# Moving sums, plain products and the second sequence's differences in a fused Fourier mixing and squared-ReLU kernel

## The chip, the cores and the metric

The kernel runs on one core of a Trainium2 chip. The metric is the device time of one execution in microseconds (us); less is better. The engines are called as in the profile: PE (TensorE), PEld (its weight loads), DVE (VectorE), ACT (ScalarE), POOL (GpSimd) and SP, whose queue issues most DMAs.

## The reference

```python
# x: (8, 3008, 256) float32; w_in: (256, 2048); w_out: (2048, 256)
X = np.fft.fft(np.fft.fft(x, axis=1), axis=2).real
t = X.reshape(8 * 3008, 256)
h = t @ w_in
out = np.square(np.maximum(h, 0.0)) @ w_out
```

Eight sequences of 3008 rows are Fourier transformed along rows and columns, the real part goes through a layer of 2048 features with a squared ReLU, and back to 256 columns.

## The kernel before

**Fourier part.** A sequence is folded on its symmetries before TensorE transforms it: sums and differences of rows (`rows_of`: sums `fs`, differences `fd`), then of columns (`columns_of`: tile `sc`, its first half from `fs`, its second from `fd`), then the split by parity (`parities_of`, which reads both halves of `sc` with a copy on ACT and writes `w`), and further halvings (`even`, `odd`, `twice_*`, `order`). The transform (`dft_ops`) gives two tables `Pt` and `Qt` for the sequence. One column of all seven later sequences is folded and transformed by itself (`fold_columns`, whose data come by small DMAs into `xe`, and `dft_ops(None)`). For the folds ACT first copies one operand into a bank of PSUM (`spare`, pool `psh`, tag h), so DVE reads one operand there.

**Layer part.** The transform along the columns is folded into w_in (`G1`, `G2`, and `gE` for the odd column). A *step* is one sequence, one block of 252 frequencies and one pair j of feature chunks; there are 6 blocks of 8 steps a sequence, 48 steps a sequence, 384 in all, numbered from 0. A step's `front` makes hP and hQ on TensorE (L984), `he` and the two halves of `g` on DVE (L988, L990, L991), ReLU and square on ACT (L995, L998). Tiles hP, hQ, the folds' banks and the transforms' banks all take turns in the two banks of `psh`: each new one waits for the reader of the one before the last.

**Products with w_out.** Two steps make a pair. POOL forms sums of their `g` (`sums_even` in even steps, L1010 to L1012; `sums_odd` in odd ones, L1020 to L1027) in tile `s`, and 20 products of a third of a step's width do the work of the 8 full ones (24 thirds) of two plain steps: 12 in `first_half` (banks F0 to F2, run three steps after the pair's even step, so in odd steps), 8 in `second_half` (banks S0 to S2, one step later). They need sums of w_out's parts (`wsum`, and some parts of `wout` replaced in place), made by `sum_wout`: a copy on ACT (L381) and three to six additions on DVE (L384), for the four groups of `SUMS`, and for pairs 0 and 1 (`slice(0, 2)`) and 2 and 3 (`slice(2, 4)`) apart. The first block (steps 0 to 7) uses w_out itself (`plain`, banks mA and mB, L1074; copied out by `gather_plain`, L1084). Every eighth step `gather` (early, upper, lower, joins) combines the banks on DVE (L1103 to L1133), and `store` transposes on DVE and writes out.

**Order of the work.** Engines run their instructions in the order in which the program issues them. The start is written out by hand in `ORDER`: TS, PW, H, PR are the four stages that round a part of w_in or w_out (`w` in front of the number: DVE, ACT, DVE, POOL); `f8b` is the TensorE half of step 8's second half, `d8b` its split on DVE (L970 to L973), `rl` and `sq` ReLU and square, `bk` the plain products of a step, `cm` POOL's sums, `sum8` and `sum9` the first sums of w_out, `hi` joins of the first sequence's transform. From step `PLAIN` = 10 on a loop issues, for each step: front, sums of w_out (up to step 14), due parts of a gather, pieces of the next sequence's folds, stores, products, ReLU, square, POOL's sums. The next sequence's pieces come from `ahead` as a list of (cost, function); `share`, `pace` and `spent` say how many of them a step may take (`FIRST` in the first sequence, `SHARE` later; `ROOM` limits a step), and pieces of no cost are issued at the end of a step (`free_pieces`). The transforms' pieces are issued between a step's products.

The list for the second sequence (sequence 1) is, before: the turning factors, 12 folds, the folds of the odd columns, their transform, 19 folds, the transforms.

Of the kernel before, what the change touches and what calls it, by code (L numbers as in the profile page):

```python
# [15 lines left out]
P = 128  # L16
# [68 lines left out]
def kernel(  # L85
# [288 lines left out]
    def sum_wout(qs, shared):  # L374
# [3 lines left out]
        ps, held = spare(slice(0, P)), {}  # L378
# [75 lines left out]
    def fold_columns():  # L454
# [12 lines left out]
        def begin():  # L467
            s = hp.tile([P, 2, NL, NE], F32, name="es", tag="es", bufs=1)
            tt(out=s, in0=xe[:, 0::2], in1=xe[:, 1::2], op=ALU.add)
            for kp in range(2):  # L470
                tt(out=we[:, :, kp], in0=s[:, 0], in1=s[:, 1], op=ALU.subtract if kp else ALU.add)
# [17 lines left out]

        def copy_pairs():  # L490
# [3 lines left out]
            nc.scalar.copy(pair, we[r, v, 1])  # L494

        def twice_even():
            butterfly(we[r, 2:3, 0], we[r, 4:5, 0], one)
            for i, u in enumerate((5, 7)):
                mix(out=we[r, u, 0], in0=we[r, u, 0], scalar=by(BY_AB, COS), in1=f[:, i], op0=ALU.mult, op1=ALU.add)

        def twice_odd():
            butterfly(we[r, v, 1], we[r, w, 1], pair)
# [68 lines left out]
    def fold_later(b):  # L571
# [5 lines left out]
        def rows_of(t):  # L577
            r = rows(t)

            def f():  # L580
# [4 lines left out]
                tt(out=fd[t][r], in0=v[r, 0::3], in1=p, op=SUB)  # L585
                load_later(LATER.index((b, t)) + NX)

            return 1.3, f

        def columns_of(t):  # L590
            r = rows(t)

            def f():
# [6 lines left out]
                tt(out=sc[t][r, :, H + 1:D], in0=q, in1=fd[t][r, :, D - 1:H:-1], op=SUB)  # L600

            return 0.8, f
# [706 lines left out]
    FIRST = (1.6, 2.6, 0.2, 0.2, 0.9, 1.9, 1.6, 1.9)  # L1309
# [10 lines left out]
    def pieces():  # L1320
# [3 lines left out]
        room, count = ROOM[i % NJ] if i >= per else 2.8, 2  # L1324
# [8 lines left out]
    def piece_beside():  # L1333
# [35 lines left out]
    def sums_at(i):  # L1369
        j, shared = i - NJ, list(SUMS)  # L1370
        if j < 3:
            for k in ((0,), (1,), (2, 3))[j]:
                sum_wout(slice(0, 2), shared[k])
        else:
            sum_wout(slice(2, 4), shared[j - 3])
# [24 lines left out]
    def step(token):  # L1400
# [45 lines left out]
        elif what == "sum":  # L1446
            sums_at(int(nm))
# [12 lines left out]
    for i in range(PLAIN, len(steps) + 7):  # L1460
        if i < len(steps):
# [10 lines left out]
            if i < NJ + 7:  # L1472
# [104 lines left out]
```

## Time and profile before

| | |
|---|---|
| three runs | 1901.33, 1901.73, 1903.04 us; median 1901.73 |
| the profiled execution | 1901.05 us, span 1899.3 us, granted clock 0.997 |
| busy, share of the span | PE 98%, PEld 92%, DVE 78%, ACT 57%, POOL 76% |
| step 10 begins at | 100.12 us of the span |
| the first sequence's last step (47) begins at | 297.54 us |
| HBM | 41.54 MB read, 24.69 MB written |

A line of the timeline holds the start, the duration, the engine, the line of the code, the operation, what it writes and reads, how many instructions are merged, and in brackets the idle time ahead of it with what ended it. A line of the waits holds who waited for whom, the total in us, how many times, and the longest. In a group of instructions the busy time and the mean duration of one (ns) stand behind the bar. In the table by stretches each engine's busy time is followed by its instructions, and the last three columns are the granted TensorE clock, the DMA share and GB/s.

### The profile page before, as it was taken

What the parts mean: (1) busy time and instruction counts of PE and PEld (TensorE: products, weight loads), DVE (VectorE), ACT (ScalarE), POOL (GpSimd) and SP (SyncE); (2) the same over time, 40 slices, a digit from 0 to 9 for tenths busy, and PEclk for the clock granted to TensorE, in tenths of its full rate; (3) what the DMA queues carried; (4) which work ended last, traced back from release to release, by engine and by line L of the source; (5) the groups of instructions that cost most, each with busy time, mean ns of one, the idle gap of its engine ahead of it and who ended that gap; (6) DMA issues with size and microseconds to landing.
All of it is one profiled execution on the core that took longest, in us unless ns stands there. A gap on an engine that the chain in (4) does not pass through costs nothing.

```text
span 1899.3 us, 34013 instructions
## 1 busy us (share of the span) xinstructions
PE 1868.8 (98%) x11408; PEld 1755.3 (92%) x11408; DVE 1478.6 (78%) x3507; ACT 1083.0 (57%) x1612; POOL 1450.8 (76%) x2115
## 2 busy tenths in 40 slices
PE   9999999999999999999999999999999999999998
PEld 7678889999999999999999999999999999999997
DVE  8688877888778877888778887788877888766665
ACT  5865655666456654656555574566645656445453
POOL 4367667887788887878778887788778878787886
PEclk9999999999999999999999999999999999999999
DMA  6431101110011000111011110111001100000000
GB/s 196 116 43 32 40 14 42 48 34 15 20 45 51 23 20 20 51 40 29 23 32 31 45 31 15 32 45 48 15 15 45 39 14 19 16 22 15 20 20 23
DMA packets 151310, 68.46 MB, mean 36 GB/s; under 512 B 131143, under 2 KB 142881, under 8 KB 151136
## 3 DMA queue, kind: packets, MB, share of 16 engines
q1 hardware_dynamic: 150590, 65.74, 13.8%
q8 instruction: 91, 1.49, 0.3%
q14 instruction: 83, 0.68, 0.1%
q0 software_dynamic: 416, 0.43, 0.1%
q10 hardware_dynamic: 130, 0.12, 0.0%
HBM read 41.54 MB, written 24.69 MB: 35 GB/s over the span
## 4 chain that ended last, share of the span: by engine, by line
PE 86%; DVE 10%; ACT 2%; issue 1%; POOL 0%; DMA 0%; SPq 0%; DVEq 0%; ACTq 0%; POOLq 0%
PE F L1045 31%; PE S L1045 19%; PE hP L984 15%; PE hQ L984 15%; DVE he L988 2%; PE pd L837 1%; PE pd L714 1%; DVE g L990 1%; DVE g L991 1%; PE mA L1074 1%; PE mB L1074 1%; PE pd L811 1%; PE pg L344 1%; ACT sp L644 1%; PE ph L955 0%
## 5 line engine op out<-in xcount | busy, mean ns | idle before, releaser
L995 ACT ACTIVATE g<-g 128x1008 f32<-128x1008 f32 (+1 forms) x384 | 399.4, 1040 | 313.7 <-DVE g L991 306.0
L988 DVE SCALAR_TENSOR_TENSOR he<-ew,gE,hP 128x252 f32<-128x252 f32 (+1 forms) x748 | 321.2, 470 | 295.9 <-PE hP L984 295.7
L998 ACT ACTIVATE g<-g 128x1008 f32<-128x1008 f32 (+1 forms) x384 | 399.3, 1040 | 12.0
L984 PE MATMUL hP<-Pt,G 128*128 128x252 f32 (+1 forms) x1496 | 380.1, 377 | 8.0 <-DVE w L646 2.9
L984 PE MATMUL hQ<-Qt,G 128*128 128x252 f32 (+3 forms) x1496 | 380.3, 377 | 5.0 <-DVE Pt L749 1.0
L1045 PE MATMUL F<-s,wsum 128*128 128x168 f32 (+1 forms) x1504 | 337.5, 306 | 0.0
L1020 POOL TENSOR_TENSOR s<-g 128x168 f32<-128x168 f32 (+1 forms) x188 | 101.8, 542 | 299.0 <-ACT g L998 294.6
L984 PEld LDWEIGHTS hQ<-Qt,G 128*128 128x128 f32 (+1 forms) x1496 | 280.2, 190 | 48.1 <-ACT g L995 4.2
L1045 PE MATMUL S<-s,wsum 128*128 128x168 f32 (+1 forms) x1504 | 305.7, 305 | 0.0
L1045 PE MATMUL F<-g,wout 128*128 128x168 f32 (+1 forms) x1504 | 305.7, 305 | 0.0
L984 PEld LDWEIGHTS hP<-Pt,G 128*128 128x128 f32 x1496 | 265.2, 190 | 29.7 <-ACT sp L631 4.3
L990 DVE TENSOR_TENSOR g<-he,hQ 128x504 f32<-128x504 f32 (+1 forms) x374 | 253.2, 677 | 49.8 <-PE hQ L984 6.2
L1045 PE MATMUL S<-s,wout 128*128 128x168 f32 (+1 forms) x1504 | 281.2, 306 | 0.1
L1045 PE MATMUL F<-g,wsum 128*128 128x168 f32 (+1 forms) x1504 | 275.0, 305 | 0.0
L1045 PEld LDWEIGHTS S<-s,wsum 128*128 128x128 f32 x1504 | 249.5, 190 | 8.2
L991 DVE TENSOR_TENSOR g<-he,hQ 128x504 f32<-128x504 f32 (+1 forms) x374 | 250.5, 670 | 0.0
L1045 PEld LDWEIGHTS F<-s,wsum 128*128 128x128 f32 x1504 | 248.8, 190 | 0.3 <-issue 0.2
L1045 PEld LDWEIGHTS F<-g,wsum 128*128 128x128 f32 x1504 | 240.6, 190 | 8.1
L1045 PEld LDWEIGHTS F<-g,wout 128*128 128x128 f32 x1504 | 240.6, 190 | 0.0
L1045 PEld LDWEIGHTS S<-s,wout 128*128 128x128 f32 x1504 | 232.1, 190 | 0.7 <-POOL s L1027 0.3
L1026 POOL TENSOR_TENSOR s<-s 128x336 f32<-128x336 f32 (+1 forms) x188 | 168.6, 897 | 14.7
L1023 POOL TENSOR_TENSOR s<-s 128x336 f32<-128x336 f32 (+1 forms) x188 | 168.5, 896 | 14.7
(227 smaller groups left out, 2498.5 us busy)
## 6 DMA issues: line engine op xcount, KB each, us to landing
out_dram<-os SPq DMA_DIRECT2D x376, 56.0 KB
xt<-in_x_dram SPq DMA_DIRECT2D x39, 384.0 KB
xt<-in_x_dram SPq DMA_DIRECT2D x63, 128.0 KB
ew<-e_dram SPq DMA_DIRECT2D x39, 126.0 KB
out_dram<-os SPq DMA_DIRECT2D x288, 7.0 KB
raw<-in_moe_w_in_dram SPq DMA_DIRECT2D x16, 256.0 KB
raw<-in_moe_w_out_dram SPq DMA_DIRECT2D x16, 256.0 KB
xt<-in_x_dram SPq DMA_DIRECT2D x2, 512.0 KB
```

The source lines that it names most:

```text
L344: nc.tensor.matmul(pg, tab[:, i], win[j][:, i], start=i == 0, stop=i == 1)
L984: nc.tensor.matmul(to[:, h, 0:n], w[:, fs], v[:, ks], start=h == 0, stop=True, skip_group_check=True)
L988: nc.vector.scalar_tensor_tensor(out=t[:, h, 0:n], in0=window[b, k0][:, 0:n], scalar=gE[:, fc:fc + 1], in1=hP[:, h, 0:n], op0=ALU.mult, op ...
L990: tt(out=g[:, :, 0:n], in0=t[:, :, 0:n], in1=hQ[:, :, 0:n], op=ALU.add)
L991: tt(out=g[:, :, n:2 * n][:, :, ::-1], in0=t[:, :, 0:n], in1=hQ[:, :, 0:n], op=ALU.subtract)
L995: act(g[:, :, 0:2 * n], g[:, :, 0:2 * n], AF.Relu)
L998: act(g[:, :, 0:2 * n], g[:, :, 0:2 * n], AF.Square)
L1020: gt(out=s[:, 11], in0=b2[:, 0], in1=b1[:, 0], op=SUB)
L1023: gt(out=s[:, 4:6], in0=s[:, 4:6], in1=s[:, 10:11].to_broadcast([P, 2, tb]), op=SUB)
L1026: gt(out=s[:, 6:9:2], in0=s[:, 2:4], in1=s[:, 6:8], op=ADD)
L1045: nc.tensor.matmul(acc[nm][:, slot, 0:tb], w, v, start=q == 0 and nm not in begun, stop=q == NJ // 2 - 1, skip_group_check=True)
L1074: nc.tensor.matmul(acc[nm][:, 0:2 * n], wout[:, j, h, c], g[:, c, 0:2 * n], start=j == c == 0, stop=j == NJ - 1 and c == 1)
```

## The change

- In `ORDER`, the plain products of steps 6 and 7 move: `bk6` to right behind `f8a`, `bk7` (before issued in the loop at step 10) to behind `rl9`.
- The sums of w_out move. Those for pairs 0 and 1 are issued one group at a time from `d6a` on (`su0a`, `su1a`, `su2a`, `su3a`) instead of at steps 8 to 10; those for pairs 2 and 3 at `su1b`, at step 10 (groups 2 and 0) and at step 11 (group 3) instead of at steps 11 to 14. Their PSUM tile comes from pool `psd` (tag d, the banks of `ends_of` and later of S1 and S2) instead of `psh`.
- `fold_columns` runs on GpSimd, but for one shuffle on DVE and the copies and multiplications on ACT.
- For the second sequence alone, `fd` and the second half of `sc` are computed on GpSimd, both operands from SBUF; ACT's copy for the latter goes.
- The second sequence's list of pieces is woven anew, with lower costs for the changed ones, and `FIRST` and the limits on a step's pieces in the first sequence differ.
- In `second_half` the third product of bank S1 comes ahead of the two of S2.

```diff
 def sum_wout(qs, shared):
-        ps, held = spare(slice(0, P)), {}
+        ps, held = psd.tile([P, 2 * D], F32, name="sw", tag="d"), {}
...
 def fold_columns():
         def begin():
             s = hp.tile([P, 2, NL, NE], F32, name="es", tag="es", bufs=1)
-            tt(out=s, in0=xe[:, 0::2], in1=xe[:, 1::2], op=ALU.add)
+            gt(out=s, in0=xe[:, 0::2], in1=xe[:, 1::2], op=ADD)
             for kp in range(2):
-                tt(out=we[:, :, kp], in0=s[:, 0], in1=s[:, 1], op=ALU.subtract if kp else ALU.add)
+                gt(out=we[:, :, kp], in0=s[:, 0], in1=s[:, 1], op=SUB if kp else ADD)
...
+        def pair_up(v, w, a):
+            gt(out=v, in0=a, in1=w, op=ADD)
+            gt(out=w, in0=a, in1=w, op=SUB)
+        def even():
             nc.scalar.copy(a, we[r, first, 0])
-        def even():
-            butterfly(we[r, first, 0], we[r, other, 0], a)
+            pair_up(we[r, first, 0], we[r, other, 0], a)
...
+        def twice_even():
             nc.scalar.copy(one, we[r, 2:3, 0])
             for i, (u, k) in enumerate(((7, SIN), (5, LESS))):
                 nc.scalar.mul(f[:, i], we[r, u, 0], by(BY_AB, k))
+            for u in (5, 7):
+                nc.scalar.mul(we[r, u, 0], we[r, u, 0], by(BY_AB, COS))
+            pair_up(we[r, 2:3, 0], we[r, 4:5, 0], one)
+            gt(out=we[r, 5:8:2, 0], in0=we[r, 5:8:2, 0], in1=f, op=ADD)
...
-        return [(0.8, begin), (0.3, order), (0.0, copy_even), (1.0, odd), (0.5, even), (0.0, copy_pairs),
-                (0.9, twice_even), (0.5, twice_odd)]
+        return [(0.1, begin), (0.3, order), (0.1, odd), (0.1, even), (0.1, odd_sums), (0.1, twice_even), (0.1, twice_odd)]
...
 def rows_of(t):
                 tt(out=fs[t][r, :, 0:D], in0=v[r, 0::3], in1=p, op=ADD)
-                tt(out=fd[t][r], in0=v[r, 0::3], in1=p, op=SUB)
+                if b == 1:
+                    gt(out=fd[t][r], in0=v[r, 0::3], in1=v[r, 1:3], op=SUB)
+                else:
+                    tt(out=fd[t][r], in0=v[r, 0::3], in1=p, op=SUB)
                 load_later(LATER.index((b, t)) + NX)
-            return 1.3, f
+            return 0.7 if b == 1 else 1.3, f
...
 def columns_of(t):
                 nc.scalar.copy(p, fs[t][r, :, 0:H + 1])
-                nc.scalar.copy(q, fd[t][r, :, 1:H])
+                if b > 1:
+                    nc.scalar.copy(q, fd[t][r, :, 1:H])
                 sc[t] = next_halves()
                 tt(out=sc[t][r, :, 0:H + 1], in0=p, in1=fs[t][r, :, D:H - 1:-1], op=ADD)
-                tt(out=sc[t][r, :, H + 1:D], in0=q, in1=fd[t][r, :, D - 1:H:-1], op=SUB)
-            return 0.8, f
+                (tt if b > 1 else gt)(out=sc[t][r, :, H + 1:D], in0=q if b > 1 else fd[t][r, :, 1:H],
+                                      in1=fd[t][r, :, D - 1:H:-1], op=SUB)
+            return 0.8 if b > 1 else 0.45, f
...
 def second_half(...):
         run((("S0", 0, 8, s[:, 2]), ("S0", 1, (0, 1), s[:, 4]), ("S0", 2, (0, 2), s[:, 8]), ("S1", 0, (1, 0), s[:, 6]),
-             ("S1", 1, 11, s[:, 10]), ("S2", 0, 7, s[:, 7]), ("S2", 1, (1, 3), s[:, 5]), ("S1", 2, 10, s[:, 3])),
+             ("S1", 1, 11, s[:, 10]), ("S1", 2, 10, s[:, 3]), ("S2", 0, 7, s[:, 7]), ("S2", 1, (1, 3), s[:, 5])),
...
 def ahead(b):
-        if b == 1:
-            early = [(0.0, start), (0.0, take_turn), (0.5, make_turn)]
-            middle = [(0.0, scale_columns)] + fold_columns() + tables + dft_ops(None)
...
-        return early + one + middle + two + groups
+        head = [(0.0, start), (0.0, take_turn), (0.5, make_turn)] + one[:9]
+        return (head + woven(one[9:] + two[:5], [(0.0, scale_columns)] + fold_columns(), 1) + tables
+                + woven(two[5:], dft_ops(None), 2) + groups)
+    def woven(ops, others, each):
+        out, others = [], list(others)
+        for k in range(0, len(ops), each):
+            out += ops[k:k + each] + others[:1]
+            del others[:1]
+        return out + others
...
-    FIRST = (1.6, 2.6, 0.2, 0.2, 0.9, 1.9, 1.6, 1.9)
+    FIRST = (1.6, 2.8, 0.0, 0.0, 0.9, 1.9, 1.6, 1.9)
...
-        room, count = ROOM[i % NJ] if i >= per else 2.8, 2
+        room, count = ROOM[i % NJ] * (1.0 if i >= per else 1.3), 2 if i >= per else 3
...
 ORDER
-        'gE6 PRw4 d6b sq5 fe7 pgC7 gE7 TSw5 bk4 TSw6 PWw5 restQ GC7 d6a spl PWw6 Hw5 f7b PRw5 f7a TSw7 bk5 Hw6 '
-        'PWw7 d7b PRw6 rl6 d7a sq6 f8b Hw7 f8a rl7 d8a sq7 PRw7 d8b sum8 rl8 f9a sq8 hi8 f9b d9a cm8 bk6 '
-        'd9b rl9 sum9 sq9 hi9 cm9 '
+        'gE6 PRw4 d6b sq5 fe7 pgC7 gE7 TSw5 bk4 TSw6 PWw5 restQ GC7 d6a su0a spl PWw6 Hw5 f7b PRw5 f7a su1a TSw7 bk5 '
+        'Hw6 PWw7 d7b PRw6 rl6 su2a d7a sq6 f8b Hw7 f8a bk6 rl7 d8b su3a PRw7 sq7 d8a rl8 f9a sq8 hi8 f9b d9a cm8 '
+        'd9b rl9 bk7 sq9 su1b hi9 cm9 '
...
 the loop
-            if i < NJ + 7:
-                sums_at(i)
+            for k in {PLAIN: (2, 0), PLAIN + 1: (3,)}.get(i, ()):
+                sums_of_wout(k, 1)
...
-        if i == PLAIN:
-            back_at(NJ - 1)
-        elif at >= NJ and at < len(steps):
+        if at >= NJ and at < len(steps):
```

More of the change, by code (lines that the diff above doesn't have):

```diff
@@ L475, in order, with odd_sums @@
             nc.vector.stream_shuffle(v, v, REVERSE)
-        def copy_even():
+        def pair_up(v, w, a):
+            gt(out=v, in0=a, in1=w, op=ADD)
+            gt(out=w, in0=a, in1=w, op=SUB)
+        def even():
             nc.scalar.copy(a, we[r, first, 0])
-        def even():
-            butterfly(we[r, first, 0], we[r, other, 0], a)
+            pair_up(we[r, first, 0], we[r, other, 0], a)
         def odd():
             for i, u in enumerate((other, first)):
-                tt(out=m[:, 3 * i:3 * i + 3], in0=we[r, u, 1], in1=turned(SIN + i, u), op=ALU.mult)
+                gt(out=m[:, 3 * i:3 * i + 3], in0=we[r, u, 1], in1=turned(SIN + i, u), op=ALU.mult)
             for u in (first, other):
-                tt(out=we[r, u, 1], in0=we[r, u, 1], in1=turned(COS, u), op=ALU.mult)
-            tt(out=we[r, both, 1], in0=we[r, both, 1], in1=m, op=ALU.add)
-        def copy_pairs():
+                gt(out=we[r, u, 1], in0=we[r, u, 1], in1=turned(COS, u), op=ALU.mult)
+        def odd_sums():
+            gt(out=we[r, both, 1], in0=we[r, both, 1], in1=m, op=ADD)
+        def twice_even():
             nc.scalar.copy(one, we[r, 2:3, 0])
@@ L493, in copy_pairs, with twice_odd @@
                 nc.scalar.mul(f[:, i], we[r, u, 0], by(BY_AB, k))
-            nc.scalar.copy(pair, we[r, v, 1])
[L496 to L502, printed above, removed]
-        return [(0.8, begin), (0.3, order), (0.0, copy_even), (1.0, odd), (0.5, even), (0.0, copy_pairs),
-                (0.9, twice_even), (0.5, twice_odd)]
+            for u in (5, 7):
+                nc.scalar.mul(we[r, u, 0], we[r, u, 0], by(BY_AB, COS))
+            pair_up(we[r, 2:3, 0], we[r, 4:5, 0], one)
+            gt(out=we[r, 5:8:2, 0], in0=we[r, 5:8:2, 0], in1=f, op=ADD)
+        def twice_odd():
+            nc.scalar.copy(pair, we[r, v, 1])
+            pair_up(we[r, v, 1], we[r, w, 1], pair)
+        return [(0.1, begin), (0.3, order), (0.1, odd), (0.1, even), (0.1, odd_sums), (0.1, twice_even), (0.1, twice_odd)]
     folds = turns = 0
@@ L1180, in ahead @@
         tables = [(0.0, lambda tab=tab, t=t: part_table(tab, t)) for t in (TWO, ODD0) for tab in (cosT, sinT)]
-        if b == 1:
-            early = [(0.0, start), (0.0, take_turn), (0.5, make_turn)]
-            middle = [(0.0, scale_columns)] + fold_columns() + tables + dft_ops(None)
-        else:
-            early, middle = [], []
-            groups = [(0.0, start)] + groups
-        one, two = fold_later(b)
-        return early + one + middle + two + groups
+        one, two = fold_later(b)
+        if b > 1:
+            return one + two + [(0.0, start)] + groups
+        head = [(0.0, start), (0.0, take_turn), (0.5, make_turn)] + one[:9]
[7 more added lines that the diff above has]
+        return out + others
     pieces = [fold(t) for t in range(NT)]
@@ L1367, in front_at, with sums_of_wout @@
         return b, k0, n, j, made["g", i]
[L1369 to L1375, printed above, removed]
+    def sums_of_wout(k, h):
+        sum_wout(slice(2 * h, 2 * h + 2), list(SUMS)[k])
     def rows_at(i):
@@ L1445, in step @@
             sums_of(int(nm))
-        elif what == "sum":
-            sums_at(int(nm))
+        elif what == "su":
+            sums_of_wout(int(nm[0]), int(nm[1] == "b"))
         elif what == "hi":
```

## The prediction

> **What bounds the kernel now.** First the page: who is busy, and at which clock.
>
> ```profile
> PE 1868.8 (98%) x11408; PEld 1755.3 (92%) x11408; DVE 1478.6 (78%) x3507; ACT 1083.0 (57%) x1612; POOL 1450.8 (76%) x2115
> PEclk9999999999999999999999999999999999999999
> ```
>
> TensorE (PE) is the bound, 30.5 us short of the span. The table by stretches says where they lie (us, PE, PEld, DVE, ACT, POOL busy).
>
> ```profile
> 80.00:100.00 20.00, 16.61 (x44) 9.35 (x43) 14.26 (x36) 13.65 (x19) 7.86 (x9) 0.83 0.40 67
> 100.00:120.00 20.00, 19.45 (x100) 15.83 (x99) 16.87 (x46) 11.36 (x28) 13.77 (x20) 1.00 0.35 22
> 120.00:142.00 22.00, 19.82 (x117) 17.62 (x116) 19.41 (x43) 15.88 (x28) 15.89 (x24) 1.00 0.48 69
> 183.00:252.00 69.00, 62.90 (x379) 56.94 (x378) 59.96 (x148) 42.85 (x78) 47.10 (x70) 1.00 0.11 30
> 302.00:529.00 227.00, 226.37 (x1412) 216.26 (x1411) 181.96 (x428) 131.31 (x194) 180.44 (x264) 1.00 0.12 32
> ```
>
> From 302 us on PE lacks 0.6 us in 227: next to nothing to win there. Up to then the timeline, read from one first hP to the next, gives each step. Unhindered, an odd step lasts 5.13 us (two fronts 1.71, 24 matmuls of F 3.42), an even one 3.98 (16 of S, 2.28). In the first sequence steps 12 to 17 lose 4.7 us (0.8, 1.4, 1.4, 0.4, 0.6, 0.1) and steps 18 to 47 lose 13.1 (19 1.2, 21 0.4, 25 0.7, 27 1.7, 28 1.1, 32 0.6, 33 0.9, 34 2.1, 36 0.6, 37 1.1, 38 0.2, 39 0.4, 43 2.1), the transforms' own matmuls (0.95 or 0.86 a hook) taken off; steps 48 to 95, with the same folds for the third sequence spread thinner, lose 2.0 together. The waits (total, times, longest) name the cause: the two banks of tag h go round in order, so hP or hQ waits for the bank that a fold of the next sequence took.
>
> ```profile
> PE hP L984 <- DVE fd L585: 1.9, 4, 0.8
> ...
> PE hP L984 <- DVE w L615: 1.9, 1, 1.9
> ```
>
> Ahead of that stands one hole, with a slow stretch behind it.
>
> ```profile
> 90.98 0.69 PE L955 MATMUL ph<-Pt,G 128*128 128x252 f32 x2 [2.63 <-DVE g L973]
> ...
> 92.97 1.21 PE L955 MATMUL ph<-Pt,G 128*128 128x252 f32 x2 [0.76 <-DVE wout L384]
> ...
> 94.82 1.88 PE L1074 MATMUL mA<-g,wout 128*128 128x504 f32 x2
> ```
>
> 3.4 us idle in all, then matmuls at half clock: the last halves take 1.85 instead of 0.85, the eight products of step 6 5.3 (94.82 to 100.12) instead of 3.4: 2.9 us.
>
> **Part 1, the start.** Products of steps 6 and 7 move ahead of where PE waits; at best hole and slow stretch go, -6.3. But the sums of w_out move up in DVE's and ACT's queues, past the rounding of w_out, and I laid the queues out with the trace's durations. Sum 0 (six operations, 2.1) starts at 81.0, ahead of Hw5 (80.35 before), so Hw5 ends at 83.7, PRw5 (1.50 on POOL) at 85.3, and the products of step 5, which need it, begin at 85.4, not 83.1: a new hole of 2.3. TSw7 waits for PRw5's buffer, PWw7 (ACT 2.1) ends at 87.9, rl6 at 89.0, and only then comes the copy of sum 2; DVE waits for it and does split 7a at 90.5 to 91.7 (85.0 to 86.3 before). That is a second hole, 2.2, ahead of f8a. Products 6 and 7 run at 92.6 to 96.0 and 97.7 to 101.1, step 10's front by 102.8 (with product 7, 105.2 before): PE gains 2.4, the others lose. Split 9b ends at 99.4 (96.3); the copies of mA and mB now stand ahead of sq9 on ACT, sq9 ends at 103.0; the last early sum waits for its copy until 103.5; step 10's he starts at 105.4 (101.2); nine more sum operations (3.2) put step 11's he at 111.3 (106.3). Its F starts at 108.4 (106.9). Steps 12 to 14 carry no sums any more (before, 10 operations), their banks no longer stand between the fronts' (waits by L384 before: 0.8, 0.4), and step 14 starts at 123.3 (121.67): **+1.6**, between -6.3 and +4.5 (1.6 and one slow stretch of 2.9). I take the layout's value, since each link of it is a duration of this trace. Sum 3 of the second half frees S2's bank at 114.4, S2's turn comes 1.7 later: hidden.
>
> A rule to weigh here: in the trace an idle 2.63 and 0.76 us, 0.9 apart, was enough for the half clock. [...]
>
> **Part 2, differences on GpSimd.** Rows:
>
> ```profile
> L585 DVE TENSOR_TENSOR fd<-xt,sp 96x512 f32<-96x512 f32 x6 | 4.1, 677 | 0.0
> L600 DVE TENSOR_TENSOR sc<-sp,fd 96x254 f32<-96x254 f32 x6 | 2.5, 410 | 0.0
> ...
> L1209 POOL TENSOR_TENSOR sc<-xt 128x512 f32<-128x512 f32 x1 | 1.3, 1303 | 10.5 <-DMA raw<-in_moe_w_in_dram 10.5
> L1211 POOL TENSOR_TENSOR sc<-sc 128x256 f32<-128x256 f32 x1 | 0.7, 682 | 0.1
> ```
>
> DVE loses 8 x 0.68 and 8 x 0.41, and some 5.5 of the columns' folds (160 to 171 us): 14 us. POOL gains 8 x 1.30 and 8 x 0.68, and 15 to 17 small operations; no row has them: 0.2 (128x2 memsets cost 0.13) to 0.7 (a 1x1 copy) each, I take 0.3 (slope of 168 to 336 elements): 21 us in all. POOL's own sums take 2.0 in an even and 5.9 in an odd step:
>
> ```profile
> 123.09 0.54 POOL L1020 TENSOR_TENSOR s<-g 128x168 f32<-128x168 f32 x1 [2.16 <-ACT g L998]
> ...
> 128.50 0.54 POOL L1027 TENSOR_TENSOR s<-s,g 128x168 f32<-128x168 f32 x1
> ```
>
> So POOL has 9.12 - 7.9 = 1.2 a pair to spare. S needs the sums some 5 us after they end (step 13's end at 129.0, their S begins at 134.3), which hides a late POOL from PE; not from the parities, though, whose ACT copies read the half of sc that POOL now writes. With the new costs the pacing (44.6 units over 45.6 shares, 0.978 a share) gives step 12 make_turn and rows(2), step 13 rows(3), columns(2), rows(0), step 14 columns(3) and at once parities(2, 3). POOL then does: odd sums of 11, from 115.6 (111.6 before) to 121.5; rows(2) 122.8; even sums 124.8; rows(3), columns(2), rows(0) 128.1; odd sums of 13 134.0; columns(3) 134.7. Copy 0.4, two DVE operations 0.75: the bank comes free at 136.0, and step 15's hQ, 128.24 before, starts then. That is +7.8, of it 1.6 from part 1: **+6.2**. Queued behind on ACT stand relu and square of step 14, on DVE step 15's he. Were POOL not behind at all, odd sums from square 13 (6.9 after step 13's start) would still cost 2.2; 8 is the upper end. PE stands idle 7.8 us, so the half clock comes again; what is left of it when work resumes, half to all of the 6.9 seen (91.5 to 98.4), costs half its length, 1.7 to 3.4: **+2.5**. Steps 16 and 17 then lose 0.1, not 0.7: **-0.6**. The other three parities stand one or two steps behind their columns: no wait. ACT saves eight copies (0.37 each); the next load of x on SP now waits for POOL (rows(2): 122.8, where SP before got to it at 128.2 anyway), and behind it the columns' loads, last issued before at 140.8, wanted at the end of step 16, about 148: hidden.
>
> **Part 3, spreading.** FIRST gives steps 2 and 3 of a block nothing (there the gathers' 1.8, 2.1 and 2.3 fill DVE), the columns' folds are woven between the second sequence's from step 17 on, and from step 18 on 9.2 us of DVE are gone (3 x 0.68, 4 x 0.41, 5.5). The pacing leaves 18, 19, 26 to 28, 34 to 36, 42 and 43 without a piece. I take what steps 48 to 95 lose, 2.0, instead of 13.1: **-11.1**. The heavy steps left (29, 31 to 33, 37) could keep 5, so -8; all gone is -13.1. What hides the folds left is DVE's room, 2.9 us in an odd step (5.13 less its own 2.2) and 1.8 in an even one.
>
> **Part 4, order of S.** Only the end is exposed:
>
> ```profile
> 1889.56 0.44 PE L1045 MATMUL S<-s,wsum 128*128 128x164 f32 x2
> ...
> 1890.11 0.50 DVE L1113 TENSOR_TENSOR vt<-S,cs 128x328 f32<-128x328 f32 x1 [0.75 <-PE S L1045]
> ```
>
> vt waits for S1's last product, which moves two places up; then S2 bounds the second addition, at 1890.1, not 1890.64: **-0.5** (0 at worst).
>
> Sum: 1.6 + 6.2 + 2.5 - 0.6 - 11.1 - 0.5 = -1.9. The profiled run took 1901.05 (span 1899.3 and 1.75 around it), so 1899.2 for it; the median is 0.68 higher: 1899.8. 0.2% (3.8 us) is about what a measurement can tell from no change.
>
> **Rivals.** Forecast, 0.37: gain and new wait nearly cancel; own range 1895.5 to 1903.5 (0.13 faster, 0.21 same, 0.03 slower).
> Faster, 0.26: the sums fit DVE's idle time (1.7 at 81.0, 1.5 at 86.9), start -3.4, and POOL is on time, so the wait costs 2.2: -3.4 + 2.2 + 2.5 - 0.6 - 11.1 - 0.5 = -10.9, 1890.8. For it: DVE is busy only 14.26 of 20 there. Against: sum 0 stands ahead of Hw5.
> Slower, 0.30: POOL becomes the bound of steps 12 to 25. Own sums 7 x 7.9 = 55.3, folds 10.4 + 4.8, small ones 5 at 0.3: 75.5, against PE's 65.7 (7 x 9.12 + 1.9 of transforms) and the 10.3 (7.8 + 2.5) it is held anyway: just even. At 0.7 each the small ones cost 6.4 more, on PE too, since the cover of 5 us is used up by then, and a hole of that length halves the clock once more, 1.7 at least: 1899.8 + 8.1 = 1907.9. For it: 85% of POOL's time is taken in a steady pair. Against: all but one of the small ones are at most 56 elements wide. It decides from about 0.33 us an operation.
> The plain products don't do what is said, 0.07: the new holes slow the clock at the start too, 1902.7 (0.04 same, 0.03 slower).
> Together: faster 0.39, same 0.27 (0.02 of the slower rival's), slower 0.34. The range leaves out one in ten at each side: 1889.5 to 1908.5.
>
> **What would show it.** Right: PE idle some 7 us between the S of step 14 and hQ of step 15, released by w L615, ACT's copy L610 ahead of it released by POOL; half clock behind; two holes near 84 and 90; no L585 wait; steps 18 to 47 losing 2 to 5. Wrong: no hole at step 15 (faster rival), POOL idle nowhere from 120 to 185 us (slower), or losses in 18 to 47 as before.

## The result and the profile after

| | before | after |
|---|---|---|
| median of six runs | 1901.32 us (1900.73 to 1903.04) | 1911.93 us (1910.45 to 1914.14) |
| ratio | | 1.0055, 95% interval 1.0042 to 1.0068 |
| span of the profiled execution | 1899.3 us | 1908.7 us |
| step 14 / 18 / 48 begins | 121.67 / 142.41 / 302.58 us | 124.50 / 151.43 / 310.87 us |
| first step of sequence 7 / last hP to the end | 1664.14 us / 22.6 us | 1674.30 us / 21.9 us |

The change made the kernel about 10.6 us slower; 1899.8 us was forecast, with a range up to 1908.5. Cut at the steps of the table, the 9.5 us of span are: +2.8 up to step 14, +6.2 in steps 14 to 17, -0.7 in steps 18 to 47, +1.9 in sequences 1 to 6 and -0.7 from sequence 7 on. The page shows less DVE and more POOL, as meant, and a clock that fell in one slice of 48 us, the third:

```profile
PE 1870.7 (98%) x11408; PEld 1760.7 (92%) x11408; DVE 1468.4 (77%) x3475; ACT 1082.2 (57%) x1606; POOL 1470.7 (77%) x2146
...
PEclk9989999999999999999999999999999999999999
```

In the table by stretches (PE, PEld, DVE, ACT, POOL busy, clock, DMA share, GB/s) PE lost most from 100 to 142 us, where it had 39.3 us of work in 42 before, at full clock:

```profile
80.00:100.00 20.00, 17.56 (x50) 9.62 (x50) 15.44 (x40) 12.64 (x20) 6.46 (x6) 0.91 0.32 67
100.00:120.00 20.00, 15.96 (x71) 13.66 (x69) 15.88 (x40) 11.18 (x28) 12.45 (x18) 0.83 0.30 19
120.00:142.00 22.00, 14.99 (x82) 13.97 (x83) 11.23 (x25) 11.04 (x18) 17.68 (x23) 0.84 0.47 71
...
183.00:252.00 69.00, 62.72 (x377) 57.61 (x378) 52.54 (x131) 41.38 (x78) 51.56 (x77) 0.98 0.12 27
```

In the last line DVE is 7.4 us less busy than before, and PE does as little in 69 us as it did then (62.90): DVE's relief reached nobody. The waits of PE (total, times, longest) no longer hold the two lines shown of before; in their place stand fewer and longer ones:

```profile
PE hQ L991 <- DVE w L622: 6.9, 1, 6.9
PE hP L991 <- DVE he L995: 3.4, 1, 3.4
...
PE pd L721 <- DVE w L566: 2.5, 1, 2.5
PE mA L1081 <- POOL wout L322: 2.4, 1, 2.4
PE pd L721 <- DVE g L998: 2.0, 2, 1.0
```

(L991 was L984 before, L622 L615, L617 L610, L1052 L1045, L1081 L1074.) The longest, in the timeline:

```profile
133.17 0.54 POOL L1034 TENSOR_TENSOR s<-s,g 128x168 f32<-128x168 f32 x1
133.66 0.72 POOL L606 TENSOR_TENSOR sc<-fd 96x254 f32<-96x254 f32 x1
134.42 0.37 ACT L617 COPY sp<-sc 96x256 f32<-96x256 f32 x1 [6.11 <-POOL sc L606]
...
134.82 1.42 DVE L622 TENSOR_TENSOR w<-sp,sc 96x256 f32<-96x256 f32 x4 [6.67 <-ACT sp L617]
...
136.39 2.02 PE L991 MATMUL hQ<-Qt,G 127*128 127x252 f32 x4 [6.88 <-DVE w L622]
...
138.20 1.33 PE L1052 MATMUL F<-g,wsum 128*128 128x168 f32 x4
```

This is the chain that the prediction laid out, link by link: the odd sums end (L1034), columns(3), which is `columns_of` for tile 3 (the other pieces are named in the same way), has its turn on POOL, ACT copies, DVE splits, PE's bank comes free. Behind it four matmuls of hQ take 2.02 us instead of 1.01 and four of F 1.33 instead of 0.73: half clock (granted 0.50 from 136.4 to 139 us). The start:

```profile
85.34 2.05 PE L1081 MATMUL mA<-g,wout 128*128 128x504 f32 x2 [2.37 <-POOL wout L322]
...
106.12 2.05 PE L991 MATMUL hP<-Pt,G 128*128 128x252 f32 x4 [3.42 <-DVE he L995]
```

mA's first two matmuls and hP's four run at half clock behind their hole (granted 0.50 at 85.34 to 87 and 106.12 to 108 us). From step 18 on, two new kinds of wait:

```profile
186.69 0.37 ACT L601 COPY sp<-fs 96x258 f32<-96x258 f32 x1
...
187.10 0.42 DVE L605 TENSOR_TENSOR sc<-sp,fs 96x258 f32<-96x258 f32 x1 [4.29 <-ACT sp L601]
...
187.57 1.12 PE L991 MATMUL hP<-Pt,G 128*128 128x252 f32 x4
```

In step 24 the copy of columns(7) stands on ACT behind 4.1 us of `part_table` copies (182.70 to 186.79), and hP of step 25 comes behind both. And in step 29, in the middle of the products of F:

```profile
212.85 0.49 PE L721 MATMUL pd<-cosT,we 95*7 95x94 f32 x4 [2.48 <-DVE w L566]
...
213.99 0.45 PE L1052 MATMUL F<-g,wout 128*128 128x168 f32 x2
```

The odd columns' transform wants a bank whose fold DVE has not finished. (A transform's *hook* is the place among a step's products where a piece of a transform is issued.)

### The profile page after: what moved, and what is told of

Read it like the earlier page. It is cut to its first block, busy times and chain, and to the rows that moved or that the text cites. A ratio compares the mean times of both kernels' runs of the same rounds, so it can differ in the third digit from the quotient of the medians.

```text
span 1908.7 us, 34069 instructions
## 1 busy us (share of the span) xinstructions
PE 1870.7 (98%) x11408; PEld 1760.7 (92%) x11408; DVE 1468.4 (77%) x3475; ACT 1082.2 (57%) x1606; POOL 1470.7 (77%) x2146
## 4 chain that ended last, share of the span: by engine, by line
PE 81%; DVE 9%; POOL 2%; ACT 1%; issue 1%; SPq 0%; DMA 0%; DVEq 0%; ACTq 0%; POOLq 0%
PE F L1052 30%; PE S L1052 19%; PE hP L991 15%; PE hQ L991 14%; DVE he L995 2%; PE pd L844 1%; DVE g L997 1%; DVE g L998 1%; PE pd L721 1%; PE pd L818 1%; ACT sp L651 1%; DVE vt L1121 0%; DVE w L653 0%; DVE vt L1120 0%; DVE S L1126 0%
## 5 line engine op out<-in xcount | busy, mean ns | idle before, releaser
L991 PE MATMUL hQ<-Qt,G 128*128 128x252 f32 (+3 forms) x1496 | 381.2, 378 | 8.4 <-DVE w L622 6.9
L991 PE MATMUL hP<-Pt,G 128*128 128x252 f32 (+1 forms) x1496 | 381.1, 377 | 7.4 <-DVE he L995 3.4
L1052 PE MATMUL F<-s,wsum 128*128 128x168 f32 (+1 forms) x1504 | 338.2, 307 | 0.0
L991 PEld LDWEIGHTS hQ<-Qt,G 128*128 128x128 f32 (+1 forms) x1496 | 282.4, 191 | 48.0 <-issue 9.7
L1052 PE MATMUL F<-g,wout 128*128 128x168 f32 (+1 forms) x1504 | 306.0, 306 | 0.0
L991 PEld LDWEIGHTS hP<-Pt,G 128*128 128x128 f32 x1496 | 265.8, 190 | 29.1 <-ACT sp L638 4.3
L1052 PE MATMUL S<-s,wout 128*128 128x168 f32 (+1 forms) x1504 | 281.7, 307 | 0.1
L1052 PE MATMUL F<-g,wsum 128*128 128x168 f32 (+1 forms) x1504 | 276.1, 306 | 0.0
L1052 PE MATMUL S<-s,wsum 128*128 128x168 f32 (+1 forms) x1504 | 275.9, 306 | 0.0
L1052 PEld LDWEIGHTS F<-s,wsum 128*128 128x128 f32 x1504 | 249.6, 191 | 0.5 <-issue 0.5
L1052 PEld LDWEIGHTS F<-g,wsum 128*128 128x128 f32 x1504 | 241.7, 191 | 8.3
L1052 PEld LDWEIGHTS S<-s,wsum 128*128 128x128 f32 x1504 | 241.3, 191 | 8.2 <-issue 0.2
L1052 PEld LDWEIGHTS F<-g,wout 128*128 128x128 f32 x1504 | 241.0, 190 | 0.0
L1052 PEld LDWEIGHTS S<-s,wout 128*128 128x128 f32 x1504 | 232.7, 190 | 0.5 <-POOL s L1034 0.4
```

Source lines behind the costliest of these rows:

```text
L991: nc.tensor.matmul(to[:, h, 0:n], w[:, fs], v[:, ks], start=h == 0, stop=True, skip_group_check=True)
L1052: nc.tensor.matmul(acc[nm][:, slot, 0:tb], w, v, start=q == 0 and nm not in begun, stop=q == NJ // 2 - 1, skip_group_check=True)
```

## The experiments

All times are medians, ratios are to the kernel before in the same comparison (its median was 1900.4 to 1900.8 us there). The edits are to the changed kernel where nothing else is said. "Loses" means the time of a step over 5.13 (odd) or 3.98 us (even), less 0.95 or 0.86 for a transform's hook.

| run | us | ratio | 95% interval |
|---|---|---|---|
| e1 columns(3) early | 1909.16 | 1.0045 | 1.0033 to 1.0058 |
| e2 tables early | 1910.71 | 1.0050 | 1.0036 to 1.0064 |
| e3 transform alone | 1907.73 | 1.0033 | 1.0020 to 1.0046 |
| e4 old kernel, new start | 1902.91 | 1.0011 | 1.0003 to 1.0020 |
| e5 old order of S | 1912.44 | 1.0059 | 1.0044 to 1.0074 |
| e6 e1, scaling late | 1911.55 | 1.0059 | 1.0043 to 1.0076 |
| e7 e6, first folds on DVE | 1907.68 | 1.0034 | 1.0022 to 1.0046 |
| e8 first combination | 1899.37 | 0.9991 | 0.9982 to 1.0001 |
| e9 planned steps | 1903.82 | 1.0016 | 1.0006 to 1.0025 |
| e10 e9, first folds on DVE | 1903.97 | 1.0016 | 1.0007 to 1.0024 |
| e11 e9, new start | 1905.71 | 1.0030 | 1.0019 to 1.0040 |
| e12 planned again | 1896.11 | 0.9976 | 0.9966 to 0.9986 |
| e13 hooks late | 1907.62 | 1.0039 | 1.0026 to 1.0052 |
| e14 e12, halves on DVE | 1890.42 | 0.9940 | 0.9927 to 0.9954 |

### What makes the hole of step 15 (e1, e6, e7)

e1:

```diff
-        one = [R(TWO), R(TWO + 1), C(TWO), R(0), C(TWO + 1), both(TWO, TWO + 1), ...
+        one = [R(TWO), R(TWO + 1), C(TWO), C(TWO + 1), R(0), both(TWO, TWO + 1), ...
```

> The changed kernel, with one piece of the second sequence's list put earlier: columns(3) ahead of rows(0). By the pacing columns(3) then falls in step 13, ahead of POOL's odd sums of step 13, rows(0) in step 14 and parities(2, 3) in step 15. Theory A (the 6.88 us hole ahead of step 15's hQ comes from columns(3) standing behind POOL's odd sums in the very step in which the parities read it): the hole and the half clock behind it go, 6 to 8.7 us less than the changed kernel's 1911.9, so 1903.2 to 1906, no idle time of PE over 2 us between steps 14 and 17. Theory B (POOL as a whole is behind in steps 12 to 25): the wait comes back at the next parities, less than 3 us gained, 1909 or more.

Step 15 lasts 5.12 us instead of 13.83, so the place in POOL's queue makes that hole. But only some 2 us were gained, by theory B's number: step 18 begins at 147.48, 4 us earlier than in the changed kernel, behind a new hole of 5.62 us, and half clock follows that one too.

```profile
145.84 0.39 ACT L452 ACTIVATE xe<-xe 128x224 f32<-128x224 f32 x1 [7.42 <-DMA xe<-in_x_dram]
...
147.48 2.05 PE L991 MATMUL hP<-Pt,G 128*128 128x252 f32 x4 [5.62 <-DVE fs L586]
```

The scaling of the odd columns (ACT, end of step 16) now comes before their data. The hole of step 15 had hidden that transfer: in the changed kernel the scaling runs at 147.73, with no wait for the data. e6 keeps e1's edit and takes this wait away:

```diff
-        return (head + woven(one[9:] + two[:5], [(0.0, scale_columns)] + fold_columns(), 1) + tables
-                + woven(two[5:], dft_ops(None), 2) + groups)
+        rest, cols, odd_ops = one[9:] + two[:5], fold_columns(), dft_ops(None)
+        rest = rest[:6] + [(0.0, scale_columns), rest[6]] + cols[:2] + [rest[7]] + cols[2:4] + cols[4:] + tables
+        return head + rest + woven(two[5:], odd_ops, 2) + groups
```

> The first experiment (columns(3) early) with the scaling of the odd columns' data, which made ACT wait 7.4 us for their loads at the end of step 16, moved to the end of step 20, and the column folds behind it. Theory A (those loads alone made the new hole of step 17): no hole at steps 17 and 18, 8 us less than the first experiment's 1909.2: 1901 to 1903. Theory B (POOL is behind: at step 17 it still has to do the odd sums of step 15, and columns(4) stands behind them until 144.5 us): parities(0, 4) make a hole of 4 to 6 us in step 17, half clock behind it, and only 1 to 3 us are gained, 1906 to 1908.

```profile
142.84 0.54 POOL L1034 TENSOR_TENSOR s<-s,g 128x168 f32<-128x168 f32 x1
143.34 1.40 POOL L606 TENSOR_TENSOR sc<-fd 95x254 f32<-95x254 f32 x2
144.09 0.37 ACT L617 COPY sp<-sc 95x256 f32<-95x256 f32 x1 [4.78 <-POOL sc L606]
...
146.74 2.02 PE L991 MATMUL hP<-Pt,G 128*128 128x252 f32 x4 [4.67 <-DVE w L622]
```

Theory B's hole, at its place and of its size: the same chain as at step 15, one pair of steps later. The total came out higher than either theory had it, since the new list put a shuffle on DVE (L475) into the step of its producer on POOL and made a hole of 3.09 us ahead of step 23; e8 shows that wait. e7 leaves all pieces in their steps and takes work off POOL:

```diff
-                if b == 1:
+                if b == 1 and t not in (0, TWO, TWO + 1):
                     gt(out=fd[t][r], in0=v[r, 0::3], in1=v[r, 1:3], op=SUB)
...
+                on_dve = b > 1 or t in (0, TWO, TWO + 1, av)
...
-                (tt if b > 1 else gt)(out=sc[t][r, :, H + 1:D], ...
+                (tt if on_dve else gt)(out=sc[t][r, :, H + 1:D], ...
```

> The kernel of e6 with the differences of rows(2), rows(3), rows(0) and the second halves of columns(2), (3), (0), (4) on DVE again (with ACT's copy, as before the change); the pacing's costs are left as they are, so no piece changes its step. Theory B (POOL's backlog in steps 12 to 17 makes the holes): no hole over 2 us in steps 14 to 18, steps 12 to 17 lose 3 to 5 us in small waits as before the change; 1902 to 1905. Theory A (POOL is not what makes the holes): no gain over e6, or slower by DVE's 5 us.

No hole over 1.3 us is left in steps 12 to 18, and step 18 begins at 143.93 (146.74 in e6, 151.43 in the changed kernel). So POOL's backlog made the holes. The total missed the expected range by 2.7 us; the hole ahead of step 23, which stayed, is worth more (steps 22 and 23 lose 5.0).

### Where the gain of steps 18 to 47 went (e2, e3, e13)

e2:

```diff
-        return (head + woven(one[9:] + two[:5], [(0.0, scale_columns)] + fold_columns(), 1) + tables
-                + woven(two[5:], dft_ops(None), 2) + groups)
+        first = woven(one[9:] + two[:5], [(0.0, scale_columns)] + fold_columns(), 1)
+        return head + first[:5] + tables + first[5:] + woven(two[5:], dft_ops(None), 2) + groups
```

> The changed kernel, with the four part_table pieces (ACT copies, no cost) moved from ahead of order(5), where they are issued at the end of step 23, to behind parities(0, 4), where they are issued at the end of step 17, with no fold in steps 18 and 19. Nothing else in the list changes its step. Theory A (step 24 loses 3.8 us since columns(7)'s copy stands behind 4.1 us of table copies on ACT): step 24 loses less than 1, the time is 3 to 4 us below 1911.9, so 1908 to 1909. Theory B (step 24 loses to the transform's hook and the folds of the same step): less than 1 us, 1911 or more.

Step 24 gained 2.7 us, and yet the total moved by less than a measurement can tell. From the end of step 17 on the table copies stand ahead of a gather's copy on ACT, and step 20 loses 1.3 (DVE's vt L1120 waits 1.19 for ACT's cs). The rest was taken by the clock. The same hole of 2.48 us in step 29 as in the changed kernel was followed here by a slow stretch, which cost 1.7:

```profile
212.00 0.49 PE L721 MATMUL pd<-cosT,we 95*7 95x94 f32 x4 [2.48 <-DVE w L566]
...
213.22 0.77 PE L1052 MATMUL F<-g,wout 128*128 128x168 f32 x2
```

0.77 for two matmuls, against 0.45 above. e3:

```diff
-                + woven(two[5:], dft_ops(None), 2) + groups)
+                + dft_ops(None) + two[5:] + groups)
```

> The changed kernel, with the odd columns' transform not woven between the folds: its four hooks come first (steps 24, 25, 28, 29, without a fold in them), the folds from order(5) on behind it (steps 30 to 37). Theory A (a fold in the step of a transform's hook makes PE wait in the middle of the step, since the hook's bank and the fold's bank are next to each other in the ring): the waits of L721 in steps 24, 25, 29, 31 (0.8, 0.9, 2.5, 1.0) and step 24's wait behind the table copies (3.8 with the hook's) go, two or three of the folds that are now denser cost 1 or 2: 4 to 7 us less than 1911.9, so 1905 to 1908. Theory B (what is lost in steps 18 to 47 goes by the amount of folding alone): the losses move to steps 30 to 37, less than 1.5 us gained, 1910.4 or more.

Steps 18 to 47 took 155.9 us instead of 159.4, and the total lies at the slow end of theory A's range. More was not gained since the tables still stand ahead of step 24 (it loses 2.6) and the denser folds lose 2.2 in step 33 and 1.7 in step 38. e13 keeps every piece in its step and moves only the hook within it:

```diff
-            hook = (2, piece_beside)
+            hook = (2 if i > 37 else 8 if i % 2 else 5, piece_beside)
```

> The changed kernel, with the transforms' hooks in steps up to 37 behind the eighth product of F or the fifth of S instead of behind the second, nothing else moved. Theory A (in steps 24, 25, 29, 31, 37 PE waits in the middle of the step, since the hook's bank is the next in the ring behind the fold's, whose DVE work is not done): the waits of L721 shrink by 1.7 us (odd steps) or 0.85 (even), 4 to 5 us less than the changed kernel: 1906 to 1908. Theory B (the hook's late reading then holds the next step's hP, or DVE is full anyway): less than 1.5 us gained.

The time lies in theory A's range; by the ratios and by steps 18 to 47 (156.4 us instead of 159.4) some 3 us were gained, a little less than expected: steps 29, 31 and 37 lose 0.8, 0 and 0 instead of 2.5, 1.1 and 1.3, step 24 gains nothing, and step 25 loses 0.7 more. The waits in the middle of a step are shown to come from the hook's place.

### The start and the order of S (e4, e5)

e4 is the kernel before with the changed `ORDER`, `su` pieces and PSUM tile alone.

> The kernel before with only the changed start: order of the plain products of steps 6 and 7, the sums of w_out moved up and in the banks of the ends. Theory A (the changed start loses what the traces show between the kernels at step 14's begin, 2.8 us): 1904.1, half clock in the products of step 5 and in step 11. Theory B (most of that loss comes from the folds of steps 10 to 14, which differ too; the start alone gains a little as the sums leave steps 12 to 14): 1900 to 1902.

Between the theories. Step 14 begins 1.7 us later than before (123.37), step 18 0.6 (142.98), step 48 0.5: both holes and a slow clock are there, but the steps without sums lose 3.4 us less in 12 to 17 and give most of it back. The total is 2.1 us up (0.6 to 3.8); in the traces 1.1 lies behind the last hP, where the last transposes (1.94 us instead of 1.47) and the last transfer took longer with no change to them.

```diff
 e5
-             ("S1", 1, 11, s[:, 10]), ("S1", 2, 10, s[:, 3]), ("S2", 0, 7, s[:, 7]), ("S2", 1, (1, 3), s[:, 5])),
+             ("S1", 1, 11, s[:, 10]), ("S2", 0, 7, s[:, 7]), ("S2", 1, (1, 3), s[:, 5]), ("S1", 2, 10, s[:, 3])),
```

> The changed kernel with second_half's products in the old order (the third product of S1 behind the two of S2). Theory A (the new order costs 0.3 us in each later sequence, seen as 227.2 instead of 226.85 from one sequence's first step to the next): sequences 1 to 6 take 226.85 each again, 1.9 us less in all, and the end is 0.5 longer: about 1.4 below the changed kernel. Theory B (the 0.3 comes from something else in the change): sequences stay at 227.2, the time is the changed kernel's or 0.5 above.

By the trace, theory A: four of the six sequences take 226.82 to 226.84 us, as before, two 227.17 and 227.19 (in the kernel before two took 227.09 and 227.17); in the changed kernel five took 227.17 to 227.19 and one 227.52. Sequence 1 shows where it lies: six steps (60, 61, 76, 77, 84 and 92) each last 0.03 to 0.08 us longer in the changed kernel than in e5. The total does not show it: steps 15, 25 and 29, with whose holes the order of S has nothing to do, took 4.5 us more than in the changed kernel; the mean granted clock of the profiled execution was 0.992, against 0.993.

### Can the folds be placed on POOL? (e8 to e12, e14)

e8 puts together what the runs had shown so far.

> What the runs so far point to, together: the old start; the kernel of e7's folds; the odd columns' transform ahead of the folds from order(5) on (steps 24, 25, 28, 29); the part_table pieces spread over the ends of steps 21 to 23; the new order of S in the last pair alone. Steps 12 to 17 as before the change (losing 4.7), steps 18 to 47 losing 5 to 8 instead of 13, the end 0.5 shorter: 5 to 8 us below the kernel before, 1893 to 1896. If POOL's share of the folds were still too large, a hole of over 2 us behind a parities would show after step 18, and the time would be 1898 or more.

It missed by 3.4 us and is the same as before within the measurement. Steps 12 to 17 lose 7.5 us instead of 4.7: PE waits 1.21 us ahead of step 13 and 1.27 in it, and half clock follows. One more hole and the slow clock behind it cost as much as the whole expected gain (steps 22 and 23 lose 6.3). The time is that of the expectation's last sentence, but this hole does not stand behind a parities:

```profile
166.66 0.56 POOL L471 TENSOR_TENSOR we<-es 128x56 f32<-128x56 f32 x2
...
167.26 0.01 DVE L475 LOAD_MASK_SELECT we<-we  x1 [5.36 <-POOL we L471]
...
170.39 2.02 PE L992 MATMUL hP<-Pt,G 128*128 128x252 f32 x4 [3.10 <-DVE g L999]
```

The first fold of the odd columns was issued in step 21 and its reader on DVE in the same step; on POOL it stood behind the sums of steps 19 and 20, two halves of sc and one fd. e9 therefore fixes each piece's step by hand, by POOL's queue:

```diff
+    PLANNED = {12: 2, 13: 3, 14: 1, 15: 2, 16: 1, 17: 3, 19: 1, 20: 2, 21: 3, 22: 3, 23: 5, 30: 3, ...
...
+        if i < per:
+            for _ in range(PLANNED.get(i, 0)):
+                side.pop(0)[1]()
```

> The folds on POOL as in the change, with the old start, the new order of S in the last pair alone, and the second sequence's pieces at fixed steps. The rule: what POOL computes in an even step stands behind the odd sums and is ready only near the end of the next odd step, so POOL's pieces go into odd steps, or their readers two steps later; no piece in the gathers' steps 2 and 3 of a block; the part_table pieces one a step at the ends of steps 20 to 23; the odd columns' transform alone in steps 24, 25, 28, 29. Theory B (holes come from POOL's queue where a reader follows too closely): no hole of PE over 1.3 us from step 14 to 47, steps 12 to 17 lose 2 to 3 (4.7 before), steps 18 to 47 4 to 6 (13 before): 1891 to 1895. Rival (POOL simply has too much work by then): holes over 2 us in steps 15, 21 or 23 again, 1899 or more.

Steps 14 to 23 and 25 to 47 lose 0.8 and 5 us with no hole over 1.3, as theory B said; steps 12 and 13 lose 4.7, more than expected. The time is the rival's, but the hole stands in step 24, not in 15, 21 or 23 where the rival looked for it, and the amount of work is not its reason: five pieces shared step 23, and in e10, with less work on POOL, it stays (7.75 us).

```profile
174.39 0.22 POOL L478 TENSOR_TENSOR we<-xe,we 94x21 f32<-94x21 f32 x1
174.64 0.20 ACT L495 COPY xe<-we 94x7 f32<-94x7 f32 x1 [7.99 <-POOL we L478]
...
178.30 2.05 PE L991 MATMUL hQ<-Qt,G 127*128 127x252 f32 x4 [8.25 <-DVE w L622]
```

A copy of 7 elements on ACT read what a 0.22 us operation on POOL writes, which had its turn 8 us late. Step 24 lost 10.0 us; less that, 1903.8 would be 1893.8 (a sum, not a run). Two variants of e9 were run beside it.

> As e9, with the differences of rows(2), rows(3), rows(0) and the second halves of columns(2), (3) on DVE. Theory B (at these steps POOL's part is ready in time in e9): 1 to 2 us slower than e9, as DVE has 4.4 us more to do in steps 12 to 15, where w_out's sums are too. Rival (POOL too full): faster than e9 by 2 or more.

Step 18 begins 1.4 us later than in e9 (142.75, 141.39), as theory B said; step 48 begins 2.1 us later. The totals are even since the later sequences and the end, where the two kernels are the same, took 1.8 us less. Not the rival's gain.

> As e9, with the changed start (plain products of steps 6 and 7 earlier, sums of w_out earlier and in the banks of the ends). Theory A (the start loses its 3.4 us hole ahead of step 11 and a slow clock behind it, and gives back part of that since no sums are left in steps 12 to 14): 0.5 to 3 us slower than e9. Rival (with the folds in order, the emptier steps 12 to 14 outweigh it): faster than e9.

1.9 us slower: by theory A's number, but not by its way. Step 18 begins only 0.4 us later; the hole of step 24 grew to 10.16 us. What this comparison says of the start alone is those 0.4 us. e12 spreads the odd columns' folds and moves their transform to steps 28 to 31:

```diff
+    PLANNED = {12: 1, 13: 2, 14: 1, 15: 2, 16: 1, 17: 3, 19: 1, 20: 2, 21: 2, 22: 2, 23: 3, 24: 2, 25: 3, 28: 1, ...
```

> e9 with one lesson more: ACT's copies for the odd columns' later folds read what POOL wrote, and in e9 they stood one step behind POOL's queue and held ACT for 8 us ahead of step 24. Here those folds are spread over steps 20 to 25, their transform moves to steps 28 to 31, each hook behind the eighth (odd steps) or fifth product instead of the second, and rows(2) and columns(2), (3) to steps 13 to 15. Theory B (readers too close to POOL's queue make the holes): no hole over 1.3 us from step 12 to 47, about 8 to 11 us less than e9's 1903.8: 1893 to 1896. Rival: another hole behind parities in steps 17 to 29: 1899 or more.

Faster than both kernels, at the slow end of theory B's range. Of the edit's parts (the spreading, the later hooks, the new steps) none was run alone on e9. Steps 12 to 17 lose 2.2 us (4.7 before). Against the expectation, one hole over 1.3 us was left, and it is of a new kind:

```profile
190.29 0.54 POOL L1034 TENSOR_TENSOR s<-s,g 128x168 f32<-128x168 f32 x1
...
190.88 1.36 PE L1052 MATMUL S<-s,wout 128*128 128x168 f32 x4 [2.14 <-POOL s L1034]
```

Here PE waits for POOL's own sums: the cover between the sums and S is used up. That is the mechanism of the prediction's slower rival, POOL as the bound, seen for the first time. e14 takes six halves of sc, 4.4 us in all, off POOL, four of them (2.9) ahead of it, and leaves every piece in its step:

```diff
+                on_dve = b > 1 or t not in (TWO, TWO + 1)
...
-                (tt if b > 1 else gt)(out=sc[t][r, :, H + 1:D], ...
+                (tt if on_dve else gt)(out=sc[t][r, :, H + 1:D], ...
```

> e12 with the second half of sc on DVE again (with ACT's copy) for the six columns behind (2) and (3); fd and the odd columns' folds stay on POOL. In e12 one hole was left: in step 28 the S products waited 2.14 us for POOL's last odd sum, and a slow clock came behind it. Theory C (POOL's backlog of steps 23 to 27 has used up the 5 us that hide it from PE): with 2.8 us taken off POOL by then the wait and the slow clock go, 3 to 4 us less than e12's 1896.1, of which DVE's six operations and ACT's six copies may take 1 back: 1892 to 1894. Rival (the wait in step 28 comes from ACT's late square there, not from POOL's load): no gain, 1896 or more.

```profile
PE 1866.3 (99%) x11408; PEld 1756.9 (93%) x11408; DVE 1468.4 (78%) x3481; ACT 1082.0 (57%) x1612; POOL 1464.9 (78%) x2140
...
186.80 0.54 POOL L1035 TENSOR_TENSOR s<-s,g 128x168 f32<-128x168 f32 x1
```

```profile
100.00:120.00 20.00, 19.45 (x102) 15.98 (x102) 17.39 (x47) 11.53 (x29) 13.68 (x20) 1.00 0.36 25
120.00:142.00 22.00, 21.62 (x130) 20.23 (x129) 16.62 (x37) 15.52 (x25) 21.21 (x29) 1.00 0.49 71
142.00:183.00 41.00, 41.00 (x253) 39.18 (x252) 33.19 (x81) 30.24 (x57) 39.04 (x66) 1.00 0.21 56
```

The pair's last sum (now L1035) ends at 187.34, and S does not wait; the granted clock is 1.00 in each of these stretches. 1890.4 us, 5.7 below e12 and 10.2 below the kernel before. The edit's own part is as expected: steps 18 to 47 took 3.5 us less than in e12 (step 28 gave 3.4, steps 24 to 26 another 0.6, steps 31 and 32 took 0.5 back). That the total is better than expected is luck: in the traces 0.5 lies before step 12 and 1.2 behind step 48, where the two are the same. Theory C holds. From 120 to 183 us POOL is busy 60.2 of 63 us, which leaves little room for more on it.

## Why the prediction was wrong

The span was forecast to shrink by 1.9 us and grew by 9.5. Of these 11.4 us the spreading, which did not come, is 10.4, and the order of S in the later sequences 1.9; the start, the wait and the end together are 0.9 the other way.

**The start, +1.6: +2.8, and +1.8 to +2.0 in three more executions of the same code.** The layout of the queues was right: step 10 at 101.1 laid out and 100.8 found, its he at 105.4 and 105.2. The 1.6 has the clock whole behind both new holes, which no trace of before shows, and for the first of them it was not: half clock follows the hole of 2.37 us ahead of the products of step 5. It follows the one of 3.42 ahead of step 11 too, which the layout contains, and F of step 11 began at 109.6, not at 108.4. The half clock cost little here, though. The second hole, 2.2 us near 90 by the layout, came out at 0.2, since the slow products fill it: in e1, e2 and e13, where the clock stayed whole there, 1.57 or 1.58 us of it are seen, and step 10 begins at most 0.2 earlier. And e4, with the same half clock in step 11, which loses 3.1 us there, loses nothing in steps 12 and 13 and begins step 14 at 123.37, where the layout had 123.3. In the changed kernel's profiled execution 1.0 more is lost in step 13, where hQ waits 0.75 for a fold. e2, e3 and e13 have the same code up to step 17; they lose 3.3 us in steps 11 to 13, not 4.1, and begin step 14 at 123.46, 123.51 and 123.67. So the term was right in size, and 4.5, with one slow stretch more, would have been too much.

**The wait at step 14/15, +6.2, with +2.5 for the clock and -0.6 behind it: +6.2 in all, against 8.1.** Right in kind, place and releaser: hQ laid out for 136.0, found at 136.39. Step 14 itself began 1.2 later than laid out, so less of that belongs to this term, and the half clock cost 1.8. In e2, e3 and e13, with the same code and an earlier step 14, hQ begins at 136.10 to 136.31 and steps 14 to 17 cost 7.9, 7.7 and 8.4 more than before (the line is e2's):

```profile
136.10 2.02 PE L991 MATMUL hQ<-Qt,G 127*128 127x252 f32 x4 [7.64 <-DVE w L622]
```

That is the forecast's 8.1. Both terms together, 9.7, were found as 9.0, 9.7, 9.5 and 10.3. e1, e6 and e7 show the cause.

**The spreading, -11.1: -0.7.** This is the step that failed, by 10.4 us. The old waits did go: nothing is lost any more in steps 19, 21, 27, 28, 36, 39 and 43. What was wrong is the row taken for the rest, the 2.0 us that steps 48 to 95 lose. The third sequence's list has no tables and no odd columns' transform among its folds, and the second sequence's has both. Steps 24, 25, 29, 31 and 37 lost 3.8, 1.2, 2.5, 1.1 and 1.3 us by that. The prediction said that the heavy steps (29, 31 to 33, 37) could keep 5, and they lost 6.1, but its sum held 2.0 for all steps, and steps 24 and 25 were not among the heavy ones. It priced DVE's room in a step and not what stands behind what: a copy behind the tables on ACT, a hook's bank behind a fold's. e13 and e3 show the second (3 to 4 us). For the first, e2 shows only that its place matters, not a gain: step 24 loses 2.7 less, step 20 1.3 more. With both mended, and the transform's hooks late, e14 takes 153.5 us for steps 18 to 47, 6.7 less than before; the remaining 4.4 of the 11.1 were reached by no run.

**The order of S, -0.5 at the end: found, -0.5.** vt waits 0.21 us instead of 0.75; the other 0.2 of the end's 0.7 goes with the transposes' clock (1.06 us instead of 1.47). In the changed kernel:

```profile
1899.72 0.50 DVE L1120 TENSOR_TENSOR vt<-S,cs 128x328 f32<-128x328 f32 x1 [0.21 <-PE S L1052]
```

"Only the end is exposed" was wrong: the order cost some 0.3 us in each of six later sequences, 1.7 to 1.9 in all. e5 shows that it is the order; why these steps last longer stays open.

**The rivals.** The slower one named the right engine and the wrong price: the small operations take 0.2 to 0.42 us, all but one below the 0.33 from which it was to decide, and POOL's sums never held PE in the changed kernel. POOL was the limit all the same: its queue held ACT (6.11 us in the changed kernel, 4.78 in e6, 7.99 in e9) and DVE (5.36 in e8) long before its amount of work held PE, which the prediction had priced at step 15 alone, and the amount held PE once nothing else did (2.14 us in e12, no wait there in e14). The faster rival's start, where the sums fit DVE's idle time, was not seen.

## What to carry to other kernels

A piece moved to a less busy engine has to be priced at its place in that engine's queue: count what stands ahead of it there, and put every reader behind that, or the reader's whole queue (here ACT's, then DVE's, then TensorE's bank) stops for it, however small the piece is: in e9 ACT stood 7.99 us, DVE 9.63 and PE 8.25 behind operations of some 0.2 us. The waits that were removed here gave place to whatever was hidden beside them (in e1 ACT waited 7.42 us for a load and PE 5.62), so price a new list of pieces by its own neighbours (tables, hooks, transfers), not by another stage's total. Here the kernel got faster than before only once each piece's step was set by POOL's queue (4.3 us, e12), and most once about a quarter of the load moved to POOL, 4.4 us, was given back as well (10.2, e14). No run has this plan of steps with all folds on DVE, so how much of the gain comes from the move to POOL and how much from the plan alone is not shown.

## What was not expected of the hardware

The clock after one and the same hole is not the same from one execution to another. The hole ahead of the products of step 5, 2.35 to 2.37 us, stands in ten kernels that are alike up to there: in the profiled executions of e1, e2 and e13 it was followed by full clock (mA's first two matmuls take some 1.1 us), in those of the changed kernel, e4, e5, e6, e7 and e11 by half clock for 3 to 4 us, and in that of e3 the clock fell only in the second of the four products. The hole of 2.48 us in step 29 was followed by full clock in the changed kernel, e1, e6 and e7, by half clock in e2 and e5. The last transposes, behind 3.10 or 3.11 us, took 1.06 or 1.07 us in the changed kernel, e2, e6, e7 and e10, 1.22 in e8, 1.52 in e11 and 1.94 in e1, e3, e9, e12, e13 and e14. In the steps read here the slow matmuls behind a hole cost PE nothing (step 29 of the changed kernel), 1.7 us (step 29 of e2), 1.8 (step 15 of the changed kernel) or 3.1 (its step 11), so effects below that, as those of e2, e4 and e5, are read from the steps of a trace and not from the total. In the start, where another engine set the pace, the slow matmuls of step 5 were partly hidden: the hole behind them was 0.2 us, against 1.57 where the clock stayed whole.
